# Opening steps in a fixed engine order, and attention steps in pairs over two MLP tasks, in a fused attention and two-MLP kernel

## The chip, the cores and the metric

One core of one Trainium2 chip runs the whole program. The metric is the device time of one execution in microseconds (us). TensorE multiplies matrices (PE in the rows; PEld is its loading of weights), VectorE is DVE, ScalarE is ACT, GpSimd is POOL, and SyncE (SP) issues most DMAs.

## What is computed

The reference, cut to what matters: sliding-window attention with a linear position bias, then an MLP with ELU, then an MLP with leaky ReLU, all in float32 (the weights arrive as 64-bit words).

```python
B, H, S, D = 4, 8, 576, 64
scores = q @ k.T / sqrt(D) + slope[h] * -|i - j|      # only 0 <= i - j < 128
attn = exp(scores - max); attn /= attn.sum() + 1e-9
x = (attn @ v)                                          # 2304 tokens x 512
h = x @ w_in;  g = where(h > 0, h, exp(min(h, 0)) - 1); x = g @ w_out     # 512 -> 2048 -> 512
h = x @ w_in2; g = maximum(0.01 * h, h);                out = g @ w_out2
```

## The kernel before, in words

**Attention steps.** The 2304 tokens are cut into nine blocks of 256, each block has four pairs of heads, and each pair of heads two steps (a tile of 128 queries, or two of 64): 72 steps. A step is a chain over all engines. TensorE makes the scores s_ps of both heads (`scores`, line 102 is the matmul helper). VectorE adds the bias and takes the row minimum of the negated scores in one pass per head (line 282), and folds the two halves of the window (line 294). ScalarE does the exponential with its sum (line 296). VectorE adds 1e-9 (line 299) and takes the reciprocal (line 300); POOL normalises t (line 302). TensorE transposes t (line 333, into pt_ps), ScalarE copies that to pt (line 338), POOL cuts the triangles out by two selects (lines 348, 350), and TensorE multiplies by v (`values`, av_ps). ScalarE then writes the high part of x (line 391) and VectorE the low part (line 392).

**The opening.** The first 16 steps (two blocks) run before any MLP work. In each, four warming products are issued ahead of the transposes, and the loop is `transposes(i)`, `values_to(i - 1)`, `scores(i + 2)`. At steps 6, 9, 12 and 15 `w_tick` adds a stage of weight conversion.

**Weights.** Each of the 16 pieces of a layer (wraw, 1 MB of 64-bit words) is turned into two float32r halves w in three stages: ScalarE splits off two words (lines 153, 154), VectorE shifts and adds them (lines 162, 163), ScalarE casts the high part (line 169), and VectorE and POOL subtract for the low part (line 173). One `w_tick` per task of the first block does the rest.

**First MLP.** It runs in blocks of 512, 256, 512, 512 and 512 tokens, of 16 tasks each. A task makes h_ps of one 128-wide chunk (`mlp1_h`: 12 products into the one bank of tag h), then ELU: an exponential on ScalarE (line 419), two VectorE operations (lines 420, 421, the second of which is the last to read the bank), a cast to gh (line 422) and a difference gl (line 424). Two tasks later `mlp1_y` multiplies by w_out (12 products, y). Beside each of the first four blocks run the attention steps of the next: 8 steps in the first block, 16 in each of the others; a step has `values` and `scores` ahead of the task's h and `transposes` behind it. Everything after that (last block, second MLP) has no attention.

**Who sets the order.** Matrix products, transposes and ScalarE's two first weight operations are kept in the order of the program. On the other engines a scheduler orders the instructions at build time by priority and estimated readiness; on the chip each engine works its list strictly one after the other. Banks are handed on by tag: the transposes and the values beside the MLP share one bank, c.

## Time and profile before

| | |
|---|---|
| median of 3 runs | 1001.73 us (1001.36 to 1003.89) |
| the profiled execution | 1004.1 us, its span 1002.4 us |
| busy of the span | PE 960.7 us, DVE 417.3, ACT 404.9, POOL 233.9 |
| opening | 0 to 70 us |
| first MLP, blocks 1 to 4 beside attention | 70 to about 520 us |

The span runs from the first to the last instruction of the program, and all times in the rows count from its start. TensorE's busy time is modelled from overlapping products, so a row of several products is best read by the distance to the start of the next row. Spans on POOL are rough. Idle time stands in brackets, with the instruction that ended it.

### The profile page before, as it was taken

How to read it: one execution, taken by the hardware profiler on the slowest of the kernel's cores; microseconds unless marked ns; L12 is line 12 of the kernel's file. 1: busy time of each engine (PE TensorE's matmuls, PEld its weight loads, DVE VectorE, ACT ScalarE, POOL GpSimd, SP SyncE). 2: the span in 40 equal slices, each digit the busy share in tenths (PEclk: the TensorE clock that was granted, in tenths of full speed). 3: DMA queues.
4: the chain of work that ended last, by engine and by line, in shares of the span. 5: the costliest groups of instructions: out<-in, count | busy, mean ns of one | idle time of the engine just before them, and what ended most of it. 6: DMA issues, size and time to landing. Idle time of an engine off the chain costs nothing.

```text
span 1002.4 us, 13318 instructions
## 1 busy us (share of the span) xinstructions
PE 960.7 (96%) x4885; PEld 754.8 (75%) x4885; DVE 417.3 (42%) x1050; ACT 404.9 (40%) x927; POOL 233.9 (23%) x393
## 2 busy tenths in 40 slices
PE   7778989989999999999999999999999999999998
PEld 4346767777777777777777888888888888888886
DVE  4558776454554444444437666621121121111111
ACT  3557665334443333433337566632231222212221
POOL 3465453233333432323313233200000000000000
PEclk9769998999999999999999999999999999999999
DMA  8732121121121111210042433510020001001001
GB/s 300 267 136 80 64 92 64 35 87 49 57 63 43 30 34 33 78 35 16 1 148 84 168 126 127 168 42 22 1 84 1 1 1 43 0 1 43 1 1 42
DMA packets 41617, 66.79 MB, mean 67 GB/s; under 512 B 3664, under 2 KB 26960, under 8 KB 41552
## 3 DMA queue, kind: packets, MB, share of 16 engines
q1 hardware_dynamic: 38704, 61.22, 18.2%
q10 hardware_dynamic: 2848, 4.72, 1.4%
q8 instruction: 38, 0.62, 0.3%
q14 instruction: 27, 0.22, 0.1%
HBM read 56.49 MB, written 9.44 MB: 66 GB/s over the span
## 4 chain that ended last, share of the span: by engine, by line
PE 83%; DVE 7%; ACT 4%; POOL 2%; issue 2%; DMA 0%; ACTq 0%; DVEq 0%; POOLq 0%
PE h_ps L102 36%; PE o_y L102 17%; PE y L102 16%; PE av_ps L102 5%; PE s_ps L102 4%; PE pt_ps L333 2%; DVE t L282 2%; POOL t L302 2%; DVE w L173 1%; ACT wf L153 1%; DVE eg L420 1%; PE o_s L102 1%; PE o_c L102 1%; ACT wraw L154 1%; ACT t L296 1%
## 5 line engine op out<-in xcount | busy, mean ns | idle before, releaser
L102 PE MATMUL h_ps<-x,w 128*128 128x512 f32 (+1 forms) x1920 | 434.1, 376 | 12.1 <-DVE eg L421 10.6
L102 PEld LDWEIGHTS h_ps<-x,w 128*128 128x128 f32 x1920 | 337.2, 190 | 90.4 <-issue 13.6
L543 DVE TENSOR_TENSOR g2l<-g,g2h 128x512 fp32r<-128x512 f32 (+1 forms) x80 | 52.1, 652 | 268.6 <-ACT g2h L542 268.6
L102 PE MATMUL y<-gh,w 128*128 128x512 f32 (+1 forms) x640 | 162.9, 377 | 0.0
L102 PE MATMUL o_y<-w,g2h 128*128 128x512 f32 x512 | 157.7, 389 | 0.0
L538 ACT ACTIVATE g<-h_ps 128x512 f32<-128x512 f32 (+1 forms) x80 | 44.3, 553 | 252.1 <-PE h_ps L102 250.9
L102 PEld LDWEIGHTS y<-gh,w 128*128 128x128 f32 x640 | 110.8, 189 | 18.3 <-DVE ys L446 0.4
L302 POOL TENSOR_SCALAR t<-t,stat 128x128 f32<-128x128 f32 (+3 forms) x160 | 64.0, 413 | 213.1 <-DVE stat L300 126.4
L102 PEld LDWEIGHTS o_y<-w,g2h 128*128 128x128 f32 x512 | 96.2, 188 | 20.0
L102 PE MATMUL o_y<-w,g2l 128*128 128x512 f32 x256 | 99.7, 389 | 0.0
L296 ACT ACTIVATE t<-t,stat 128x128 f32<-128x128 f32 (+3 forms) x160 | 62.9, 394 | 79.8 <-DVE t L294 64.9
L424 POOL TENSOR_TENSOR gl<-eg,gh 128x256 fp32r<-128x256 f32 (+1 forms) x80 | 70.6, 883 | 102.8 <-ACT gh L422 90.9
L422 ACT CAST gh<-eg 128x512 fp32r<-128x512 f32 (+1 forms) x80 | 46.1, 577 | 91.1 <-DVE eg L421 91.1
L102 PE MATMUL y<-gl,w 128*128 128x512 f32 (+1 forms) x320 | 79.0, 369 | 0.0
L420 DVE TENSOR_SCALAR eg<-eg 128x512 f32<-128x512 f32 (+1 forms) x80 | 51.5, 643 | 55.7 <-ACT eg L419 55.2
L282 DVE CUSTOM_DVE_ANT_0 t<-s_ps,bias 128x256 f32<-128x256 f32 (+4 forms) x160 | 54.4, 373 | 42.1 <-PE s_ps L102 37.9
L173 POOL TENSOR_TENSOR w<-wraw,w 128x512 fp32r<-128x512 f32 x32 | 53.6, 1677 | 67.2 <-ACT w L169 67.2
L102 PEld LDWEIGHTS y<-gl,w 128*128 128x128 f32 x320 | 56.9, 189 | 10.6
L419 ACT ACTIVATE eg<-h_ps 128x512 f32<-128x512 f32 (+1 forms) x80 | 44.1, 551 | 48.7 <-PE h_ps L102 46.0
L102 PE MATMUL av_ps<-pt,vr 128*64 128x128 f32 (+2 forms) x464 | 52.8, 279 | 6.3 <-POOL pt L348 5.9
L102 PEld LDWEIGHTS o_y<-w,g2l 128*128 128x128 f32 x256 | 48.0, 188 | 9.9
L102 PEld LDWEIGHTS av_ps<-pt,vr 128*64 128x64 f32 (+1 forms) x464 | 31.5, 135 | 31.7 <-issue 17.5
(56 smaller groups left out, 816.8 us busy)
## 6 DMA issues: line engine op xcount, KB each, us to landing
wraw<-in_w_in SPq DMA_DIRECT2D x32, 512.0 KB, 3.6
wraw<-in_w_out SPq DMA_DIRECT2D x32, 512.0 KB, 4.6
qkr<-in_kT SPq DMA_DIRECT2D x28, 192.0 KB, 2.5
x2T<-ys ACTq DMA_DIRECT2D x18, 256.0 KB, 2.5
out<-os SPq DMA_DIRECT2D x18, 256.0 KB, 2.1
xr<-x2T SPq DMA_DIRECT2D x4, 1024.0 KB, 5.4
qkr<-in_qT SPq DMA_DIRECT2D x28, 128.0 KB, 2.1
vr<-in_vp SPq DMA_DIRECT2D x16, 192.0 KB, 2.5
```

The source lines that it names most:

```text
L102: tc.keep_in_program_order(nc.tensor.matmul(*args, **kw))
L173: eng.tensor_tensor(w[:, io, 1], f[:, io], w[:, io, 0].bitcast(F32), op=ALU.subtract)
L282: nc.vector.tensor_tensor_reduce(out=t[:n, c], in0=ps[hh][:n, pc], in1=bias8[:n, 2 * p + hh, P - before:P + n], scale=-D ** -0.5, scalar=3 ...
L296: nc.scalar.activation(t[:n, c], t[:n, c], AF.Exp, scale=-1.0, bias=stat[:n, 0, i:i + 1], accum_out=stat[:n, 1, i:i + 1])
L302: nc.gpsimd.tensor_scalar(t[:n, c], t[:n, c], stat[:n, 2, i:i + 1], 1.0, op0=ALU.mult, op1=ALU.mult)
L333: tc.keep_in_program_order(nc.tensor.transpose(ps[:nk, col:col + n], t[:n, c:c + nk], ident[:n, :n]))
L419: nc.scalar.activation(g[:, :m], ps, AF.Exp)
L420: nc.vector.tensor_scalar(g[:, :m], g[:, :m], 1.0, -1.0, op0=ALU.min, op1=ALU.add)
L422: nc.scalar.copy(hi[:, :m], g[:, :m])
L424: eng.tensor_tensor(lo[:, half], g[:, half], hi[:, half].bitcast(F32), op=ALU.subtract)
L538: nc.scalar.activation(g, ps, AF.Prelu, alpha=0.01)
L543: nc.vector.tensor_tensor(lo, g, hi.bitcast(F32), op=ALU.subtract)
```

## The change

`Ordered` wraps ScalarE, VectorE and POOL: while its flag is on (the opening), what they issue is kept in the order of the program. `scores` is cut into `score_mm`, `score_min`, `score_exp`, `score_rec` and `score_norm`, and the selects and the writing of x become functions of their own. The opening's loop issues these in a fixed order, with the scores three steps ahead and the reciprocal of one step between the two score passes of the next; there the 1e-9 is added on ScalarE. Three weight pieces are converted at steps given by a table, `EARLY`. Beside the MLP two steps form a pair over two tasks: values and scores of both in front of the first task, the first step's transposes behind its h, the second step's transposes in front of the second task's h. Scores of both steps share the banks s0 and s1, values of both the bank c, and x is written 256 wide. q and k have two buffers instead of three, t has four instead of three.

```diff
-W_FROM = 6
+EARLY = [(2, "a1", 0), (3, "a2", 0), (3, "ts", 0), (4, "add", 0), (5, "hi", 0), (6, "lo", 0),
+         (6, "a1", 1), (7, "a2", 1), (7, "ts", 1), (8, "add", 1), (9, "hi", 1), (10, "lo", 1),
+         (10, "a1", 2), (11, "a2", 2), (11, "ts", 2), (12, "add", 2), (13, "hi", 2), (14, "lo", 2)]
...
+                ins = f(*args, **kw)
+                if Ordered.on:
+                    tc.keep_in_program_order(ins)
...
-    rawp = attn.enter_context(tc.tile_pool(name="raw", bufs=3))
-    tp_ = attn.enter_context(tc.tile_pool(name="tp", bufs=3))
+    rawp = attn.enter_context(tc.tile_pool(name="raw", bufs=2))
+    tp_ = attn.enter_context(tc.tile_pool(name="tp", bufs=4))
...
+        for i, (t0, n, before, hh, c, pc) in enumerate(st["reg0"]):
+            dve.tensor_tensor_reduce(
+                out=t[:n, c], in0=st["ps"][hh][:n, pc], in1=bias8[:n, 2 * st["p"] + hh, P - before:P + n],
+                scale=-D ** -0.5, scalar=3.0e38, op0=ALU.add, op1=ALU.min, accum_out=stat[:n, 0, i:i + 1])
+            if i == 0:
+                between()
...
+        if Ordered.on:
+            act.activation(stat[:nq, 1, :m], stat[:nq, 1, :m], AF.Copy, bias=1e-9)
+        else:
+            dve.tensor_scalar(stat[:nq, 1, :m], stat[:nq, 1, :m], 1e-9, None, op0=ALU.add)
...
+    def scores(k):
+        if 2 * k >= NS:
+            return
+        ps = score_mm(2 * k)
+        score_mm(2 * k + 1, ps, BLK)
+        for s in (2 * k, 2 * k + 1):
+            score_min(s)
+            score_exp(s)
+            score_rec(s)
+            score_norm(s)
...
-    for i in range(FIRST):
-        transposes(i)
-        values_to(i - 1)
-        scores(i + 2)
-        if i >= W_FROM and i % 3 == W_FROM % 3:
-            w_tick(NC)
+    for n in range(FIRST):
+        m = n + 2
+        transposes(n)
+        values_to(n - 1)
+        if n + 3 < FIRST + 2:
+            score_mm(n + 3)
+        if n >= 2:
+            values_out(n - 2)
+        score_min(m, lambda: score_rec(m - 1))
+        score_norm(m - 1)
+        score_exp(m)
+        selects(n)
+        w_early(n)
...
+        todo = NPAIR * (t0 + n) // BLK - done
+        starts = [i * NC // todo + (NC // todo - 2) // 2 for i in range(todo)]
         for c in range(NC):
-            step = (c + 1) * left // NC > c * left // NC
-            if step or c == 0:
-                values_to(done - 1)
-            if step:
-                scores(done + 2)
+            if c == 0 or c in starts:
+                values_to(2 * done - 1)
+            if c in starts:
+                scores(done + 1)
+            elif c - 1 in starts:
+                transposes(2 * done + 1)
+                selects(2 * done + 1)
+                done += 1
             g = mlp1_h(J, [c])
-            if step:
-                transposes(done)
-                done += 1
+            if c in starts:
+                transposes(2 * done)
+                selects(2 * done)
```

How the order moves, at three places. VectorE in the opening, around the first writing of x, before (line 282 is the score pass and its read of the minimum, 299 and 300 the constant and the reciprocal of the step before, 392 the low part of x):

```order
L282 ISA t,stat<-s_ps,bias_87 128x128
L282 ISA stat 128x1
L282 ISA t,stat<-s_ps,bias_87 128x128
L282 ISA stat 128x1
L299 TENSOR_SCALAR stat<-stat 128x2
L300 RECIPROCAL stat<-stat 128x2
L392 TENSOR_TENSOR x_264<-av_ps,x_264 128x256
```

The same place now (line 110 is the wrapper, whatever the operation):

```order
L110 ISA t,stat<-s_ps,bias_87 128x128
L110 ISA stat 128x1
L110 RECIPROCAL stat<-stat 128x2
L110 ISA t,stat<-s_ps,bias_87 128x128
L110 ISA stat 128x1
L110 TENSOR_TENSOR x_263<-av_ps,x_263 128x256
```

The reciprocal has moved up between the two passes, and the addition of the constant has left VectorE.

TensorE in the second, 256-wide block, one step before:

```order
L102 MATMUL av_ps<-pt,vr 64x128 x4
L102 MATMUL s_ps<-qkr 128x128 x2
L102 MATMUL h_ps<-x_902,w_11_1360 128x256 x12
L333 MATMUL pt_ps<-ident,t 128x128 x2
...
L102 MATMUL y_1903<-gh,w_8_1149 128x256 x2
L102 MATMUL av_ps<-pt,vr 64x128 x4
```

and a pair of steps now:

```order
L119 MATMUL av_ps<-pt,vr 64x128 x8
L119 MATMUL s_ps<-qkr 128x256 x2
L119 MATMUL s_ps<-qkr 128x128 x2
L119 MATMUL h_ps<-x_998,w_8_1197 128x256 x12
L413 MATMUL pt_ps<-ident,t 128x128 x2
...
L119 MATMUL y_1890<-gh,w_6_1103 128x256 x2
L413 MATMUL pt_ps<-ident,t 128x128 x2
L119 MATMUL h_ps<-x_998,w_9_1240 128x256 x12
```

Values and scores of two steps stand together, the second step's transposes stand ahead of the second h, and an h and a y follow before the next values.

ScalarE in the same block, one step before (391 is the cast of x, 419 the exponential of h, 338 the copy of the transposes):

```order
L391 CAST x_1770<-av_ps 128x128
L296 ACTIVATE t,stat<-t,stat 128x128 x2
L419 ACTIVATE eg<-h_ps 128x256
L338 COPY pt<-pt_ps 128x256
L422 CAST gh<-eg 128x256
```

and a pair now:

```order
L110 CAST x_1815<-av_ps 128x256
L110 ACTIVATE t,stat<-t,stat 128x128 x4
L507 ACTIVATE eg<-h_ps 128x256
L110 COPY pt<-pt_ps 128x256 x2
L510 CAST gh<-eg 128x256
L507 ACTIVATE eg<-h_ps 128x256
```

Four exponentials of the pair stand ahead of the exponential of h, and both copies follow it.

## Rows read from the trace of the kernel before

**Rows 1.** Windows: stretch, us, busy us of PE, PEld, DVE, ACT, POOL, clock.

```profile
7.50:70.00 62.50, 48.96 (x272) 26.79 (x272) 30.20 (x134) 31.66 (x102) 31.09 (x62) 0.75 0.66 239
70.00:189.80 119.80, 109.92 (x522) 82.39 (x521) 84.67 (x161) 72.75 (x140) 52.27 (x62) 0.95 0.23 76
189.80:275.00 85.20, 78.17 (x595) 64.33 (x593) 42.69 (x175) 35.06 (x130) 28.30 (x72) 1.00 0.21 63
275.00:520.00 245.00, 245.00 (x1306) 183.33 (x1306) 109.42 (x365) 92.40 (x284) 79.82 (x159) 1.00 0.15 45
```

**Rows 2.** Waits of TensorE over the span: us in total, times, longest.

```profile
PE pt_ps L333 <- POOL t L302: 14.5, 13, 2.2
PE h_ps L102 <- DVE eg L421: 10.6, 7, 2.4
```

**Rows 3.** Timeline, TensorE, opening: start us, us, what [idle before].

```profile
24.68 0.61 PE L102 MATMUL pt_ps<-ident 128*128 128x256 bf16 x4
25.13 0.65 PE L333 MATMUL pt_ps<-ident,t 128*128 128x128 f32 x2
25.70 0.76 PE L102 MATMUL av_ps<-pt,qkvr 128*64 128x128 f32 x8
26.39 0.70 PE L102 MATMUL s_ps<-qkvr 64*128 64x256 f32 x4
...
46.82 1.13 PE L102 MATMUL av_ps<-pt,qkvr 128*64 128x128 f32 x8
```

**Rows 4.** Timeline, ScalarE, opening.

```profile
25.87 0.37 ACT L338 COPY pt<-pt_ps 128x256 f32<-128x256 f32 x1 [1.66 <-PE pt_ps L333]
26.16 0.40 ACT L296 ACTIVATE t<-t,stat 128x128 f32<-128x128 f32 x1
...
26.94 0.35 ACT L391 CAST x<-av_ps 128x256 fp32r<-128x256 f32 x1
...
30.83 1.11 ACT L153 ACTIVATE wf<-wraw 128x1024 f32<-128x1024 f32 x1
```

**Rows 5.** Timeline, VectorE, opening.

```profile
28.07 0.40 DVE L392 TENSOR_TENSOR x<-av_ps,x 128x256 fp32r<-128x256 f32 x1
...
30.82 0.42 DVE L282 CUSTOM_DVE_ANT_0 t<-s_ps,bias 128x256 f32<-128x256 f32 x1 [2.02 <-PE s_ps L102]
...
31.98 0.16 DVE L300 RECIPROCAL stat<-stat 128x2 f32<-128x2 f32 x1
```

**Rows 6.** Timeline, POOL, opening.

```profile
24.67 0.72 POOL L302 TENSOR_SCALAR t<-t,stat 128x128 f32<-128x128 f32 x2
...
30.23 0.41 POOL L348 TENSOR_SCALAR_AFFINE_SELECT pt<-pt 128x256 f32<-128x256 f32 x1 [0.92 <-ACT pt L338]
...
32.31 0.99 POOL L302 TENSOR_SCALAR t<-t,stat 128x128 f32<-128x128 f32 x2 [1.20 <-DVE stat L300]
...
59.65 2.40 POOL L302 TENSOR_SCALAR t<-t,stat 128x128 f32<-128x128 f32 x2 [2.03 <-ACT wraw L154]
```

**Rows 7.** Timeline, TensorE, first MLP block: its start, two startup waits, dearest product row.

```profile
70.04 4.09 PE L102 MATMUL h_ps<-x,w 128*128 128x512 f32 x12
...
76.80 3.06 PE L102 MATMUL h_ps<-x,w 128*128 128x512 f32 x12 [2.08 <-DVE eg L421]
...
82.62 3.67 PE L102 MATMUL h_ps<-x,w 128*128 128x512 f32 x8 [2.39 <-DVE eg L421]
...
151.50 5.49 PE L102 MATMUL h_ps<-x,w 128*128 128x512 f32 x12 [1.84 <-DVE eg L421]
```

**Rows 8.** Timeline, TensorE, one step of the 256-wide block.

```profile
218.98 1.69 PE L102 MATMUL h_ps<-x,w 128*128 128x256 f32 x12
220.50 0.38 PE L333 MATMUL pt_ps<-ident,t 128*128 128x128 f32 x2
220.64 0.72 PE L102 MATMUL y<-gh,w 128*128 128x256 f32 x4
...
223.06 1.13 PE L102 MATMUL av_ps<-pt,vr 128*64 128x128 f32 x8 [0.74 <-POOL pt L348]
```

More of the change, by code (lines that the diff above doesn't have):

```diff
@@ L46 @@
 LAG2 = 4
-def pair_of(steps, pairs, s):
-    st = steps[min(s, len(steps) - 1)]
-    return pairs.index((st["j"], st["p"]))
 def slope(h):
@@ L99, in attention_elu_leaky_kernel, with __init__, __getattr__, call @@
     nc = tc.nc
+    class Ordered:
+        on = False
+        def __init__(self, eng):
+            self.eng = eng
+        def __getattr__(self, name):
+            f = getattr(self.eng, name)
+            def call(*args, **kw):
+                ins = f(*args, **kw)
+                if Ordered.on:
+                    tc.keep_in_program_order(ins)
+                return ins
+            return call
+    act, dve, pool = Ordered(nc.scalar), Ordered(nc.vector), Ordered(nc.gpsimd)
     def matmul(*args, **kw):
@@ L255, in prep, with score_mm @@
             ahead["load"] += 1
-    def scores(s):
-        if s >= NS:
-            return
+    def score_mm(s, ps=None, at_=0):
         st = steps[s]
@@ L279, in scores, with score_min @@
             at_ += w
-        for i, (t0, n, before, hh, c, pc) in enumerate(reg):
-            nc.vector.tensor_tensor_reduce(
-                out=t[:n, c], in0=ps[hh][:n, pc], in1=bias8[:n, 2 * p + hh, P - before:P + n], scale=-D ** -0.5,
-                scalar=3.0e38, op0=ALU.add, op1=ALU.min, accum_out=stat[:n, 0, i:i + 1])
+        st["ps"], st["reg0"] = ps, reg
+        return ps
+    def score_min(s, between=lambda: None):
+        st = steps[s]
+        t = tp_.tile([P, 512], F32, tag="t", name="t")
+        stat = tp_.tile([P, 3, 4], F32, tag="stat", name="stat")
+        st["t"], st["stat"] = t, stat
+        for i, (t0, n, before, hh, c, pc) in enumerate(st["reg0"]):
[4 more added lines that the diff above has]
+                between()
@@ new lines, in score_rec, with score_norm @@
+    def score_rec(s):
+        st = steps[s]
+        nq, m = st["subs"][0][1], len(st["reg"])
+        dve.reciprocal(st["stat"][:nq, 2, :m], st["stat"][:nq, 1, :m])
+    def score_norm(s):
+        st = steps[s]
+        t, stat = st["t"], st["stat"]
+        for i, (t0, n, before, hh, c) in enumerate(st["reg"]):
+            pool.tensor_scalar(t[:n, c], t[:n, c], stat[:n, 2, i:i + 1], 1.0, op0=ALU.mult, op1=ALU.mult)
+    def scores(k):
[8 more added lines that the diff above has]
+            score_norm(s)
@@ L337, in transposes, with selects @@
             c = slice(g[0][0].start, g[-1][0].stop)
-            nc.scalar.copy(pt[:nk, c], ps[:nk, c])
+            act.copy(pt[:nk, c], ps[:nk, c])
+        st["groups"], st["col"] = groups, col
+    def selects(s):
+        if s >= NS:
+            return
+        st = steps[s]
+        pt, groups, col = st["pt"], st["groups"], st["col"]
         for (nk, m), g in groups.items():
@@ L367, in values @@
         xh, xl = X1[J]
-        whole = j < RAW
+        early = j < RAW
         pt = st["pt"]
         tiles = [x for x in st["reg"] if x[3] == 0]
-        if not whole:
-            av, off = psp.tile([P, 512], F32, tag="c", name="av_ps"), -j * BLK
-        elif st["first"]:
-            av, off = psp.tile([P, 512], F32, tag=f"y{p % 2}", name="av_ps"), -j * BLK
-            AV[p] = av
-        else:
-            av, off = AV[p], -j * BLK
+        if st["first"]:
+            AV[p] = psp.tile([P, 512], F32, tag=f"y{p % 2}" if early else "c", name="av_ps")
+        av, off = AV[p], -j * BLK
         for t0, n, before, _, _ in tiles:
@@ L386, in values, with values_out @@
                                      start=i == 0, stop=i == len(mine) - 1)
-        if whole and not st["last"]:
+        st["out"] = None
+        if st["last"]:
+            o = slice(j * BLK - BLK1[J][0], j * BLK + BLK - BLK1[J][0])
+            st["out"] = xh[:, p, o], xl[:, p, o], av[:, :BLK]
+    def values_out(s):
+        if s >= NS or not steps[s]["out"]:
             return
-        a, b = (j * BLK, j * BLK + BLK) if whole else (tiles[0][0], tiles[-1][0] + tiles[-1][1])
-        q, o = slice(a + off, b + off), slice(a - BLK1[J][0], b - BLK1[J][0])
-        nc.scalar.copy(xh[:, p, o], av[:, q])
-        nc.vector.tensor_tensor(xl[:, p, o], av[:, q], xh[:, p, o].bitcast(F32), op=ALU.subtract)
+        xh, xl, av = steps[s]["out"]
+        act.copy(xh, av)
+        dve.tensor_tensor(xl, av, xh.bitcast(F32), op=ALU.subtract)
     def mlp1_h(J, cs):
```

116 lines of the change are left out of this document (74 added, 42 removed).

## The prediction

> **What bounds the kernel now.** I read the stages first, then the waits, then the timeline of each engine inside the stages. The windows by stage [rows 1] show where TensorE is not busy: it is idle for 62.5 - 48.96 = 13.5 us of the opening (7.5 to 70 us, sixteen attention steps), 119.8 - 109.92 = 9.9 us of the first MLP block (70 to 189.8), 85.2 - 78.17 = 7.0 us of the second, 256-wide block (189.8 to 275), and never between 275 and 520. Behind 520 us the change moves nothing. So at most some 30 us are open, plus what the clock takes: the granted clock is 0.75 of 2.4 GHz in the opening, that is half of it at 1.2 GHz, and 0.95 in the first block. The waits of TensorE [rows 2] name who ends the idle time: the normalising on POOL before the transposes (opening), and the maximum on VectorE that frees the one bank of h_ps (first block).
>
> **The opening, priced as a loop.** The order listing shows what is cured: before, VectorE does the +1e-9 and the reciprocal of a step behind the next step's two score passes, which wait for that step's products. In the new order the products come a step earlier, the constant is added on ScalarE, and the reciprocal stands between the two passes. What remains is a ring of fixed orders; I add up two steps, because the output copy of a pair comes every second one, and call one trip a turn.
>
> *Ring through TensorE:* transposes to the copy's start 25.87 - 25.13 = 0.74 [rows 3, 4]; copy 26.16 - 25.87 = 0.29, x cast 0.35 [rows 4]; x subtraction 0.40, score pass 0.42 [rows 5]; reciprocal to normalising 32.31 - 31.98 = 0.33, normalising 0.72, first select 0.41 [rows 5, 6]; values 26.39 - 25.70 = 0.69, scores 0.70, the four warming products 25.13 - 24.68 = 0.45 [rows 3], and the transposes again: 5.50 us, 2.75 a step.
> *Ring through ScalarE:* copy 0.29, cast 0.35, x subtraction 0.40, pass, reciprocal, pass and minimum at 0.42 + 0.16 + 0.42 + 0.42, two exponentials 26.94 - 26.16 = 0.78, the added constant, then reciprocal, pass, minimum, exponentials and constant of the second step. The minimum has no row here and is taken as a pass. The 128x2 addition on ScalarE has none either: between 0 and the 0.40 of an exponential [rows 4], I take 0.2, being nearer to the small end by width. Sum: 3.44 + 1.98 = 5.42 us. (The Trainium skill, "ScalarE: Activation LUTs", section "What ACT_TABLE_LOAD costs", puts an ACTIVATE with immediate operands at 186 ns plus 0.833 ns per element, 0.19 us here; the sum would be the same within 0.2 us. No run here shows it yet.)
> *Weights:* nine ScalarE stages of 1.11 us [rows 4] are put at fixed steps, after the exponentials. Where one falls into the odd step only, the second copy comes 0.4 us later, and the turn is 5.8; where both steps have one (steps 5/6 and 9/10), 6.9. The stages on VectorE and POOL stand behind their step's work and are hidden by the wait for the next products; if that cover goes, they come on top (second rival).
>
> So: first transposes at 7.5 us as before, three steps at 2.75 to step 3 (15.8), six turns (4 x 5.8 + 2 x 6.9 = 37.0) to step 15 (52.8), then one last way through copy, cast, subtraction, pass, reciprocal, double normalising of the 64-row step, selects and values: 0.74 + 0.29 + 0.35 + 0.40 + 0.42 + 0.33 + 1.44 + 0.82 + 0.69 = 5.5. The first MLP product starts at 58.3 us at full clock, against 70.04 [rows 7]. At half clock values take 1.13 instead of 0.76 [rows 3]; with as much for scores and warming, a turn grows by 1.1: eight turns at that give 65. I put the clock where it was, half the time, and 1 us for passes that meet on SBUF: **62 us, -8** (bounds -11.7 and -5). The weights at hand are then three whole pieces, where before two were whole and two half done.
>
> **First MLP block.** Two startup waits of 2.08 and 2.39 us [rows 7] stay: in both orders six exponentials and two weight passes stand on ScalarE ahead of the second task's exponential. The other 9.9 - 4.5 = 5.4 us come where VectorE and ScalarE have a step's scores and a weight piece at once; the new order has four such places instead of eight, but after eight of its tasks nothing but y lies between h and the next h. I take half, 2.7 us. A clock of 0.95 over 119.8 us is worth 6.0 us of TensorE work; the dearest product row, 5.49 us for twelve products, is such a stretch behind a wait [rows 7]. With half the waits gone I give back somewhat under half: **-5** together. Bounds: -11 (both gone but the startup) and +3.1 (eight tasks with 5.4 / 14 = 0.39 us each, the mean wait of a task behind the startup, on top of what there is).
>
> **Second, 256-wide block.** Today each step's values wait 0.74 us for the select [rows 8], as only y lies between. Now h and y lie between the second step's transposes and the values, 1.52 (218.98 to 220.50) + 1.68 (220.64 to 223.06 less its wait) = 3.2 us [rows 8], so that wait goes. What is late next: ScalarE has one queue, and in most pairs four exponentials now stand ahead of exp(h), whose maximum frees the h bank. From the end of the scores: four passes and two minima on VectorE 6 x 0.42 = 2.5, the second pair of exponentials 0.78, exp(h) at most 0.40, two VectorE passes 0.84: 4.5 us. TensorE comes back to that bank after h, transposes, y, transposes: 1.52 + 0.14 + 1.68 + 0.14 = 3.5 us [rows 8]. So up to 1.0 us a pair; in some pairs a score is only 128 wide, in some the order puts exp(h) first: I take 0.6 of the 0 to 1.0, 4.8 us for eight pairs against 7.0 today: **-2** (bounds -7 and +1).
>
> **275 to 520 us.** TensorE is always busy [rows 1]; in these 512-wide tasks y alone covers the chain. Values and scores of two steps now run together: two changes between products and attention less per pair. One change costs between 0 and 0.14 us (the whole spacing of a transpose pair [rows 8]); 16 pairs: 0 to -4.5, **-1.5** taken.
>
> **No cost.** Two buffers for q and k instead of three: a pair's loads on SP now wait for scores that were read a whole pair earlier, and land during the two tasks between; on SP the sixteenth weight piece moves ahead of the eleventh and twelfth, which are used ten tasks and more later. The fourth buffer of t only removes waits. The x copies are half as many and twice as wide, off the path of the products.
>
> Sum: -8 - 5 - 2 - 1.5 = -16.5. The profiled execution took 1004.1 us (span 1002.4) and lies 2.4 above the median of the three runs, 1001.7; I subtract from the median: **985.2 us**.
>
> **Rivals.**
> 1. *Everything comes in:* full clock in the opening (-11.7), no wait behind the startup in the first block (-9), the h bank always in time (-6), changes at 0.09 us (-3): 972. For it: a shorter turn has fewer gaps, and the granted clock is 1.00 where TensorE is always busy [rows 1]. Against: the granted 0.75, in an opening with TensorE 78% busy. 20%.
> 2. *POOL and VectorE in each other's way:* POOL's normalising takes 0.72 us undisturbed and 2.40 beside weight work on VectorE [rows 6]. Three pieces have six such VectorE stages (add, subtraction); if each meets a normalising in the ring, 6 x 1.68 = 10 us: the opening ends at 72, the sum is 995. Against: the stages stand where the next normalising is not due. 15%. (The Trainium skill says in "GPSIMD Engine Reference", section "Specifications", that POOL shares its SBUF interfaces with VectorE and that instructions with two SBUF inputs contend; by that rule this is what the added piece would do. The trace agrees, 2.40 beside 0.72.)
> 3. *The pair gives back what the opening wins:* in the 256-wide block the passes, both pairs of exponentials and the two reciprocals run strictly one behind the other, 2.0 us a pair: 16 instead of 7, +9; the first block gains nothing: 1001, no change. 8%.
> 4. *Slower: a fixed order exposes every weight stage.* On queues that no longer choose, a stage that is not ready holds all behind it. Nine ScalarE stages are 10 us, the nine on VectorE bounded by the same; on half-clock turns of 6.6: 7.5 + 8 x 6.6 + 20 + 5.5 = 86 us, +16, with the rest as forecast 1009. It decides from an opening longer than 78.5 us. For it: these engines were free to be ordered around a late stage before, and from then on are not. Against: ScalarE is busy for 31.66 of the 62.5 us only [rows 1], so there is room for a late stage to be made good. 9%.
>
> That the change does not do what it says is excluded by the order: it shows both the ring and the pairs.
>
> **Numbers.** The forecast has 48%. A measurement tells about 0.3% (3 us) from no change: faster 48 + 20 + 15 and 1 from the third, 0.84; same 0.07; slower 0.09. The range reaches from below rival 1 by its unknown costs to just over rival 3: 967 to 1003, which leaves out rival 4 and the far ends. The forecast's own range, each term moved by about half of the way to its bounds, is 976 to 993.
>
> **What would show it.** Right: first MLP product near 62 us; pairs of steps 5.5 to 7 us apart in the opening, with the wait for POOL under 8 us; no wait of av_ps for POOL in the 256-wide block, and in its place h_ps waiting for VectorE under 1 us a pair. Wrong: an opening over 66 us with normalising at 1.4 us and more (rival 2), h_ps waits of 2 us a pair (rival 3), ScalarE idle ahead of a weight stage (rival 4), or waits in the 512-wide blocks, where I expect none.

## The result: 966.6 us, and the profile after

The changed kernel takes **966.62 us** (median of 4 runs, 966.46 to 968.23), the kernel before 1002.78 us (4 runs, 1001.36 to 1003.89): ratio 0.9644, 95% interval 0.9625 to 0.9663. The gain is 36 us where 16.5 were forecast; the time lies 0.4 us below the range. The profiled execution took 966.66 us, its span is 964.8. The medians below leave out one execution of e16 at 1045.2 us and one of the kernel before at 1855.5, far above the others.

The windows of the changed kernel, cut where its stages begin (columns as in [rows 1]: stretch, us, busy us of PE, PEld, DVE, ACT, POOL, clock); the last one holds the two 512-wide blocks with attention.

```profile
7.50:60.10 52.60, 40.94 (x267) 23.30 (x267) 28.38 (x113) 34.11 (x121) 31.05 (x61) 0.90 0.91 315
60.10:171.20 111.10, 106.12 (x525) 81.39 (x524) 84.22 (x158) 73.50 (x136) 51.87 (x61) 0.97 0.20 65
171.20:245.90 74.70, 71.61 (x595) 63.24 (x593) 40.95 (x166) 33.18 (x122) 28.92 (x72) 1.00 0.25 72
245.90:470.30 224.40, 223.99 (x1250) 174.92 (x1248) 99.09 (x336) 84.84 (x258) 77.81 (x156) 1.00 0.13 39
```

The last of these windows in the kernel before, same columns:

```profile
274.90:507.80 232.90, 232.90 (x1254) 173.33 (x1252) 103.96 (x353) 87.89 (x274) 78.09 (x157) 1.00 0.12 36
```

The opening is shorter by 9.9 us (the start of the first product of the MLP, from here on the opening's mark, is 60.1 for 70.0), the first block by 8.6 (111.1 for 119.7), the 256-wide block by 10.5 (74.7 for 85.2), and the two 512-wide blocks, in which TensorE showed no idle time at all, by 8.4 (in the kernel before they end at 507.8 us, inside the last window of [rows 1]). The waits of TensorE over the span answer to [rows 2]:

```profile
PE pt_ps L413 <- POOL t L110: 8.7, 13, 1.8
PE h_ps L119 <- DVE eg L509: 5.0, 10, 1.3
PE pt_ps L413 <- ACT pt L110: 4.4, 3, 2.5
PE av_ps L119 <- POOL pt L110: 3.0, 1, 3.0
```

The wait for the normalising fell by 5.8 us and that for the bank of h by 5.6; the wait for ScalarE's copies is new. The wait of the values for the selects, not among [rows 2], fell by 3.8. In the kernel before it was:

```profile
PE av_ps L102 <- POOL pt L348: 6.8, 9, 0.9
```

Together that is 15.2 us less and 4.4 more, far from 36. The timeline of TensorE in the 256-wide block shows what else changed (answers to [rows 8]):

```profile
198.57 0.64 PE L119 MATMUL y<-gh,w 128*128 128x256 f32 x4
199.14 1.15 PE L119 MATMUL av_ps<-pt,vr 128*64 128x128 f32 x16
200.22 0.92 PE L119 MATMUL s_ps<-qkr 64*128 64x256 f32 x8
201.07 1.69 PE L119 MATMUL h_ps<-x,w 128*128 128x256 f32 x12
```

Sixteen value products now take 1.08 us (199.14 to 200.22). Before, eight took 1.06 there (223.06 [rows 8] to the next start, 224.12), and 0.60 in the block's second task, where y was 512 wide (200.40 to 201.00):

```profile
200.40 0.67 PE L102 MATMUL av_ps<-pt,vr 128*64 128x128 f32 x8
201.00 0.70 PE L102 MATMUL s_ps<-qkr 64*128 64x256 f32 x4
...
224.12 0.70 PE L102 MATMUL s_ps<-qkr 64*128 64x256 f32 x4
```

### The profile page after: what moved, and what is told of

The parts are those of the page before. It is cut to its first block, busy times and chain, and to the rows that moved or that the text cites. A ratio compares the mean times of both kernels' runs of the same rounds, so it can differ in the third digit from the quotient of the medians.

```text
span 964.8 us, 13200 instructions
## 1 busy us (share of the span) xinstructions
PE 934.1 (97%) x4885; PEld 751.3 (78%) x4885; DVE 408.9 (42%) x1003; ACT 403.0 (42%) x917; POOL 234.6 (24%) x393
## 4 chain that ended last, share of the span: by engine, by line
PE 80%; DVE 3%; ACT 3%; issue 1%; DMA 0%; ACTq 0%; DVEq 0%
PE h_ps L119 37%; PE o_y L119 18%; PE y L119 16%; PE av_ps L119 4%; PE s_ps L119 3%; ACT t L110 1%; PE o_s L119 1%; PE pt_ps L413 1%; PE o_c L119 1%; DVE t L110 1%; DVE eg L508 1%; DVE eg L509 1%; ACT wraw L174 0%; ACT wf L169 0%; DVE stat L110 0%
## 5 line engine op out<-in xcount | busy, mean ns | idle before, releaser
L659 DVE TENSOR_TENSOR g2l<-g,g2h 128x512 fp32r<-128x512 f32 (+1 forms) x80 | 52.1, 653 | 268.9 <-ACT g2h L658 268.9
L119 PE MATMUL y<-gh,w 128*128 128x512 f32 (+1 forms) x640 | 160.0, 372 | 0.0
L512 POOL TENSOR_TENSOR gl<-eg,gh 128x256 fp32r<-128x256 f32 (+1 forms) x80 | 68.2, 852 | 139.8 <-ACT gh L510 132.0
L110 POOL TENSOR_SCALAR t<-t,stat 128x128 f32<-128x128 f32 (+3 forms) x160 | 65.7, 424 | 136.3 <-DVE stat L110 130.0
L508 DVE TENSOR_SCALAR eg<-eg 128x512 f32<-128x512 f32 (+1 forms) x80 | 46.8, 586 | 94.4 <-ACT eg L507 91.1
L110 ACT ACTIVATE t<-t,stat 128x128 f32<-128x128 f32 (+3 forms) x160 | 62.5, 392 | 55.2 <-DVE t L110 40.4
L512 DVE TENSOR_TENSOR gl<-eg,gh 128x256 fp32r<-128x256 f32 (+1 forms) x80 | 41.6, 521 | 39.0 <-ACT gh L510 38.8
L509 DVE TENSOR_TENSOR eg<-h_ps,eg 128x512 f32<-128x512 f32 (+1 forms) x80 | 51.1, 638 | 2.7
```

The source lines that it names most:

```text
L110: ins = f(*args, **kw)
L119: tc.keep_in_program_order(nc.tensor.matmul(*args, **kw))
L508: nc.vector.tensor_scalar(g[:, :m], g[:, :m], 1.0, -1.0, op0=ALU.min, op1=ALU.add)
L509: nc.vector.tensor_tensor(g[:, :m], ps, g[:, :m], op=ALU.max)
L512: eng.tensor_tensor(lo[:, half], g[:, half], hi[:, half].bitcast(F32), op=ALU.subtract)
L659: nc.vector.tensor_tensor(lo, g, hi.bitcast(F32), op=ALU.subtract)
```

## Experiments

All stages in us, read from TensorE's timeline: the start of the first product (the opening's end), the first block, the 256-wide block, the two 512-wide blocks; then the median time. The ratios in the text are each to executions of the kernel before taken beside the run (medians 1001.2 to 1003.1 us). The diffs are shortened, with some lines joined.

| run | opening | first | 256 | 512 x 2 | time |
|---|---|---|---|---|---|
| before | 70.0 | 119.7 | 85.2 | 232.9 | 1002.8 |
| changed | 60.1 | 111.1 | 74.7 | 224.5 | 966.6 |
| e1 pairs only | 65.6 | 111.4 | 74.6 | 224.5 | 974.0 |
| e2 opening only | 60.0 | 117.8 | 83.8 | 232.9 | 994.4 |
| e3 second select aside | 65.1 | 121.6 | 80.4 | 232.1 | 995.3 |
| e4 interleaved | 61.6 | 110.8 | 78.7 | 227.2 | 974.1 |
| e5 transposes behind | 59.6 | 115.6 | 73.7 | 224.8 | 971.5 |
| e6 transposes together | 60.9 | 111.6 | 76.8 | 232.5 | 977.9 |
| e7 buffers only | 66.1 | 121.4 | 84.4 | 232.9 | 1002.5 |
| e8 last select first | 60.2 | 109.4 | 74.7 | 224.5 | 964.9 |
| e9 before again | 65.7 | 119.7 | 85.3 | 232.9 | 1001.3 |
| e10 not pinned | 53.4 | 111.2 | 74.7 | 224.6 | 960.5 |
| e11 reciprocal behind | 62.5 | 111.4 | 74.7 | 224.5 | 969.3 |
| e12 copies behind | 59.8 | 111.1 | 72.9 | 224.3 | 965.6 |
| e13 constant on ScalarE | 65.7 | 109.3 | 74.6 | 224.5 | 970.9 |
| e14 products earlier | 56.5 | 111.0 | 74.6 | 224.5 | 963.4 |
| e15 free, together | 52.9 | 110.1 | 72.8 | 224.2 | 959.3 |
| e16 one run | 52.1 | 109.9 | 79.6 | 225.4 | 964.1 |
| e17 x behind | 54.9 | 110.1 | 74.4 | 224.5 | 959.8 |
| e18 pinned, best | 52.0 | 109.6 | 72.8 | 224.3 | 955.3 |

**Which half gains what.** Two runs take the halves of the change apart. e1 has the scheduler's old opening, then the pairs:

```diff
-    Ordered.on = True
-    ...
+    for i in range(FIRST):
+        transposes(i); selects(i); values_to(i - 1); score_one(i + 2)
+        if i >= 6 and i % 3 == 0:
+            w_tick(NC)
```

> The pairs of steps beside the MLP with the opening as it was before (scheduler's order, weight stages from step 6 on, +1e-9 on VectorE). Theory (the parts are separate): the first MLP product stays near 70 us, and the 256-wide block (-10.5 us), the two 512-wide blocks behind it (-8.5 us) and the first block (-8.6 us) gain as in the changed kernel: about 974 us. Rival (the first block gained because the new opening leaves three whole pieces of weights and a tidy start): of the 8.6 us only the fewer changes of four pairs, some 2 us, are left: about 981 us. The forecast's own terms would have given 1002 - 5 - 2 - 1.5 = 993 us.

Measured: 974.0 us, 0.9721 (0.9698 to 0.9743). e2 has the new opening, then the old loop of single steps:

```diff
-            if c in starts:
-                scores(done + 1)
+            if step:
+                score_one(done + 2)
             g = mlp1_h(J, [c])
+            if step:
+                transposes(done); selects(done); done += 1
```

> The new opening, then one attention step at a time beside the MLP, as before. Theory (separate parts): first MLP product at 60 us instead of 70, all behind it as before: 1002.8 - 10 = 993 us. Rival (the first block's gain comes from the opening): a further 6 us, 987 us. The forecast's own term was -8: 995 us.

Measured: 994.4 us, 0.9927 (0.9896 to 0.9959). The first theory holds: the halves are separate, and the pairs bring 27.5 us of the 36. Most of the first block's gain goes with the pairs too: 111.4 with the old opening, 117.8 with the new one alone.

**The 256-wide block.** In e3 the kernel before keeps its two selects, but the second writes where nobody reads (so a mask is left out), and nothing waits for it:

```diff
-            nc.gpsimd.affine_select(out=both, in_=both, pattern=[[0, 2], [1, n]], base=0,
+            aside = tp_.tile([P, 2 * P], BF16, tag="aside", name="aside", bufs=1)
+            nc.gpsimd.affine_select(out=aside[:, :w]..., in_=both, pattern=[[0, 2], [1, n]], base=0,
```

> The kernel before, in which the second select writes to a tile that nobody reads: the products of the values wait for the first select alone, and POOL has the same work. The mask of the tokens after a query is left out by this. Theory (a wait for the second select hides inside the rows of the values, which look busy): in the 256-wide block the rows of 8 value products shrink from 1.07 to about 0.60 us (start to next start), about 0.45 us in 14 of 16 steps, -6 us; in the 512-wide blocks, where the 8 take 0.59 us already, nothing; in the opening up to 0.4 us a step of the ring, 0 to -6 us: 990 to 997 us. Rival (values cost more there for another reason, such as what the products before them were): no row changes, 1002 us within 0.3%.

Measured: 995.3 us, 0.9933 (0.9908 to 0.9957), and 4.8 of it in this block (85.2 to 80.4). The timeline of e3, one step of the block:

```profile
242.59 0.67 PE L102 MATMUL av_ps<-pt,vr 128*64 128x128 f32 x8 [0.76 <-POOL pt L348]
243.18 0.49 PE L102 MATMUL s_ps<-qkr 64*128 64x128 f32 x4
```

The wait of 0.76 us for the first select is still there; the eight products behind it now take 0.59 us, not 1.06. The row that looked busy held a wait of 0.47 us for the second select, which follows the first on POOL. The trace of the kernel before had it too, not in TensorE's products but in its weight loading: at 223.53 in the row of [rows 8], when POOL's second select (223.08, 0.41 us) is done, and 3.1 us in 11 places of the block:

```profile
223.08 0.41 POOL L350 TENSOR_SCALAR_AFFINE_SELECT pt<-pt 128x256 f32<-128x256 f32 x1
223.06 0.19 PEld L102 LDWEIGHTS av_ps<-pt,vr 128*64 128x64 f32 x2 [0.95 <-POOL pt L348]
223.53 0.42 PEld L102 LDWEIGHTS av_ps<-pt,vr 128*64 128x64 f32 x6 [0.28 <-POOL pt L350]
...
PEld av_ps L102 <- POOL pt L350: 3.1, 11, 0.4
```

(The Trainium skill says in "Perfetto Trace Analysis", section "Summary: the profiler window per engine type", that the end shown for a TensorE instruction is an estimate. The trace agrees: these eight products look busy for 1.13 us with that wait and for 0.67 without it.)

**The 512-wide blocks.** e4 alternates values and scores in each pair; no place of attention is added between the products of the MLP:

```diff
-                values_to(2 * done - 1)
-                scores(done + 1)
+                values_to(2 * done - 2); ps = score_mm(2 * done + 2)
+                values_to(2 * done - 1); score_mm(2 * done + 3, ps, BLK)
```

> The changed kernel, in which the values and the score products of a pair alternate step by step (values, scores, values, scores) instead of 16 value products and then 8 score products; the number of places where attention stands between products of the MLP is the same. Theory J (every change between kinds of matmul costs): two more changes a pair; by the rows of the changed kernel 8 values cost 0.59 us at the start of a run and 0.48 behind 8 others, 4 scores 0.64 and 0.42: +0.32 us a pair, 28 pairs, +9 us: 975.5 us. Rival (only the changes between the MLP's products and attention cost): no difference, 966.6 us within 0.3%.

Measured: 974.1 us, 0.9721 (0.9700 to 0.9743): 7.5 us lost. One pair of e4's 512-wide blocks:

```profile
274.71 0.66 PE L119 MATMUL av_ps<-pt,vr 128*64 128x128 f32 x8
275.30 0.70 PE L119 MATMUL s_ps<-qkr 64*128 64x256 f32 x4
275.93 0.67 PE L119 MATMUL av_ps<-pt,vr 128*64 128x128 f32 x8
276.53 0.70 PE L119 MATMUL s_ps<-qkr 64*128 64x256 f32 x4
```

and of the changed kernel:

```profile
269.31 1.15 PE L119 MATMUL av_ps<-pt,vr 128*64 128x128 f32 x16
270.38 1.14 PE L119 MATMUL s_ps<-qkr 64*128 64x256 f32 x8
271.44 3.04 PE L119 MATMUL h_ps<-x,w 128*128 128x512 f32 x12
```

The same 24 matmuls take 2.45 us alternating (to 277.16) and 2.13 in two runs. That is 2.7 of the 8.4 us in the two blocks (and as much in the 256-wide one, beside 1.4 us more of listed waits); 16 pairs of the kind shown would give 5.1, so the other kinds gain less. The other 5.7 us lie between e2 and e4 (232.9 and 227.2): one run of values and scores fewer a pair, 0.36 us. Part of it was hidden waits here too, 0.8 us by e3 (232.9 to 232.1). The rows of pairs like the one above give the rest of the split: two steps take 14.33 us before (values at 293.27 to values at 307.60), a pair of e4 14.08 (274.71 to 288.79), a changed pair 13.76 (269.31 to 283.07). So one place of attention fewer is worth 0.25 us, and the grouping in the place that stays 0.32; an estimate for 16 pairs is 4.0 us for the places, and 0.9 of the 5.7 stays open.

**Where the second step's transposes stand.** e5 puts them behind the second task's first products:

```diff
-                transposes(2 * done + 1)
             g = mlp1_h(J, [c])
+            if c - 1 in starts:
+                transposes(2 * done + 1)
```

> The changed kernel with the second step's transposes behind the first products of the second task (as the first step's are) instead of ahead of them. Only y then lies between these transposes and the values. Theory (what the place ahead of the products buys is the cover for the selects): in the 256-wide block each pair waits again for the first select, 0.74 us, and for the second, 0.47 us, 8 pairs: up to +9.7 us; in the 512-wide blocks y takes 2.8 us and covers the chain: 0; the wait of 2.48 us at the first pair behind the opening goes: -2.5. Sum 966.6 + 7 = 974 us. Rival (the pair alone is enough, since the selects of the second step are queued on a freer POOL): 964 to 967 us.

Measured: 971.5 us, 0.9709 (0.9687 to 0.9732). Of the theory only the sum was near: the 256-wide block is 1.0 us *shorter* and no wait for a select is listed in it (one row of sixteen values takes 1.30 us, the others 1.07). So it is not h between the transposes and the values that ends that wait; the pair is enough. The loss is in the first block (115.6 for 111.1). Over the span the waits of h for VectorE are

```profile
PE h_ps L119 <- DVE eg L509: 13.6, 15, 3.4
```

against 5.0 us in the changed kernel; 8.8 us of them stand in the first block, where the changed kernel has 2.5. e6 puts the transposes of both steps into one run and one bank, where they fit:

```diff
-                transposes(2 * done + 1)
+                transposes(2 * done + 1, transposes(2 * done), width(2 * done))
```

> The changed kernel with the transposes of both steps in one run into one bank, ahead of the second task's products, where they fit the bank (20 of 28 pairs). Theory J (every place where attention stands between the products costs beside its own matmuls): by the rows of the changed kernel y behind transposes takes 2.92 us and 2.81 without, h before them 2.88 and 2.84: -0.15 us a pair, 20 pairs, -3 us, and the two waits of 0.9 us for the copy out of the transposes' bank in the 256-wide block go: -5 us in all, 961.6 us. Rival (two copies and four selects now stand between the transposes and the values, 0.6 + 1.6 us and more against 3.2 us of products in the 256-wide block, so the values wait again, up to 0.5 us in six pairs): no gain, 964 to 967 us.

Measured: 977.9 us, 0.9768 (0.9749 to 0.9786), worse by 11 us, which neither theory had. Its waits name a new one: the second step's transposes wait for the first step's copy out of the shared bank, queued on ScalarE.

```profile
PE pt_ps L419 <- ACT pt L110: 15.6, 21, 2.5
```

e12 gives the two copies out behind both runs of transposes:

```diff
-                    transposes(2 * done + 1, transposes(2 * done), width(2 * done))
+                    transposes(2 * done + 1, transposes(2 * done, alone=False), width(2 * done), alone=False)
+                    copies(2 * done); copies(2 * done + 1)
```

> The transposes of both steps in one run into one bank as in the run before, but with the two copies out of the bank given out behind both runs of transposes: there the second step's transposes waited 15.6 us in all for the first step's copy on ScalarE, which lies in the same bank. Theory J (one place less where attention stands between products gains 0.25 us, as h and y gained 4.0 us for 16 pairs of the two 512-wide blocks): those waits go, 20 pairs gain 0.15 to 0.25 us each, -3 to -5 us: 961.6 to 963.6 us, the two 512-wide blocks 221.5 to 222.7 us instead of 224.5. Rival (the values now wait for copies and selects that start later): 966 us or more, with waits of the values for POOL in the 256-wide block.

Measured: 965.6 us, 0.9644 (0.9623 to 0.9665). Those waits are gone (2.5 us are left, the one at the start); 1.8 us come in the 256-wide block, and in the 512-wide ones 0.2, not 2 to 3; the interval of the whole overlaps that of the changed kernel. Joining two places of transposes gains next to nothing: the first four products of y take 1.01 us behind transposes and 0.91 elsewhere, but four transposes in one run take 0.35 us, and two runs of two 0.13 and 0.14. Theory J holds for values and scores, not for these.

**The opening.** First, how firm its length is: e7 is the kernel before with the change's buffers, e9 the kernel before unchanged.

```diff
-    rawp = attn.enter_context(tc.tile_pool(name="raw", bufs=3))
-    tp_ = attn.enter_context(tc.tile_pool(name="tp", bufs=3))
+    rawp = attn.enter_context(tc.tile_pool(name="raw", bufs=2))
+    tp_ = attn.enter_context(tc.tile_pool(name="tp", bufs=4))
-            vr = rawp.tile([P, 4, P], F32, tag="vr", name="vr")
+            vr = rawp.tile([P, 4, P], F32, tag="vr", name="vr", bufs=3)
```

> The kernel before with the buffers of the change alone: four for t, two for q and k, three for v. In the run with pairs and the old opening the first product of the MLP started at 65.6 us, not at 70. Theory (the fourth buffer of t, which the prediction booked as removing waits at no gain, shortens the old opening, since a step's scores no longer wait for the transposes of the step three before): first product near 65.5 us, 997.5 us. Rival (the buffers change nothing; the scheduler ordered that opening otherwise because other work follows it): first product at 70 us, 1001.6 us within 0.3%.

> The kernel before once more, for its profile. In its profile the granted clock was 0.74 to 0.53 between 30 and 66 us and the first product of the MLP came at 70 us; with the buffers alone changed it was 1.00 up to 40 us and 66.1 us, at the same time of the whole. Theory (the opening before has no fixed length: how long the clock stays at half differs from one execution to the next): first product between 65 and 70 us, with a granted clock unlike that of the first profile in the opening, everything behind 190 us the same within 1 us. Rival (70 us belongs to the kernel before and 66 to the buffers): 70 us again, within 1 us.

Measured: e7 1002.5 us, 1.0009 (0.9989 to 1.0028); e9 1001.3 us, with the first product at 65.7. The buffers gain nothing. Each stage behind the opening repeats to 0.2 us, the opening itself only to 4.3: its granted clock was 0.75 [rows 1] and in the second execution

```profile
7.50:65.70 58.20, 42.49 (x272) 23.63 (x272) 30.23 (x134) 31.65 (x102) 31.24 (x62) 0.87 0.74 258
```

So the new opening is worth 5.6 to 9.9 us by its marks, 7.2 by the medians of e2 (in whose profile the first and the 256-wide block are 3.3 us shorter too). Four runs look for its cause. e10 removes the pins:

```diff
                 ins = f(*args, **kw)
-                if Ordered.on:
-                    tc.keep_in_program_order(ins)
```

> The changed kernel with the opening's instructions given out in the same sequence, but not held in it: the scheduler may order ScalarE, VectorE and POOL in the opening, as in the kernel before (+1e-9 stays on ScalarE there). Theory (the fixed order is what shortens the opening): first product at 65 us or later, some 5 us lost, 971 us and more. Rival (the products of a step earlier and the added constant on ScalarE do it, and the scheduler keeps it): first product at 60 us, 966.6 us within 0.3%.

e11 moves the reciprocal behind both passes and the minimum:

```diff
-            if i == 0:
-                between()
         st["reg"] = []
         ...
+        between()
```

> The changed kernel with the reciprocal of a step behind both score passes and the minimum of the next step on VectorE, not between the passes; the rest of the fixed order stays. Theory (the ring of the prediction: normalising waits for the reciprocal, and so for 0.42 + 0.42 us more in each step that the ring through TensorE ends): +0.84 us in each of 13 to 16 steps less what the ring through ScalarE covers, +6 to +12 us, first product at 66 to 72 us, 973 to 978 us. Rival (the ring through ScalarE or the weights set the pace): under +2 us.

Measured: e10 **960.5 us**, 0.9594 (0.9569 to 0.9620), 6.1 us *faster* than with the fixed order, which neither theory had; e11 969.3 us, 0.9678 (0.9660 to 0.9700), 2.7 us slower than the changed kernel, between theory and rival. e13 and e14 then add to e1 one part of the new sequence each, unpinned:

```diff
-        if Ordered.on:
+        if s < FIRST + 2:
             act.activation(stat[:nq, 1, :m], stat[:nq, 1, :m], AF.Copy, bias=1e-9)
```

> The run with pairs and the old opening (974.0 us, first product at 65.6), with one part of the new opening added: +1e-9 on ScalarE for the opening's steps, nothing pinned. Theory (what gains is the products of the scores a step earlier; the constant only spares VectorE a small operation): 0 to -3 us, first product at 63 to 66 us. Rival (the constant on VectorE, behind the next step's passes, is what held the normalising): first product at 57 us or earlier, 965 us.

```diff
+        if i + 3 < FIRST + 2:
+            score_mm(i + 3)
         score_one(i + 2)
```

> The run with pairs and the old opening (974.0 us, first product at 65.6), with the other part: the score products of the opening are issued one step earlier, the constant stays on VectorE, nothing pinned. Theory: -8 to -12 us, first product at 54 to 58 us, 962 to 966 us, near the run without pins (53.4 us). Rival (the products earlier gain nothing without the constant and the order on VectorE): 972 to 974 us.

Measured: e13 970.9 us, 0.9680 (0.9645 to 0.9716), 3.1 us by medians with the opening's mark unmoved and intervals that overlap; e14 963.4 us, 0.9611 (0.9581 to 0.9641): **the score products a step earlier gain 10.6 us**. VectorE's wait for score products in the opening says why: 18.3 us in e1, 6.2 in e14. In the kernel before it was

```profile
DVE t L282 <- PE s_ps L102: 29.1, 15, 3.4
```

and in that of the changed kernel, first VectorE, then ScalarE, what the fixed order put in its place:

```profile
DVE x L110 <- ACT x L110: 12.1, 6, 3.6
DVE stat L110 <- ACT stat L110: 5.0, 8, 1.0
DVE x L110 <- PE s_ps L119: 2.2, 1, 2.2
DVE t L110 <- PE s_ps L119: 0.8, 1, 0.8
...
ACT t L110 <- DVE t L110: 11.7, 8, 1.7
```

VectorE hardly waits for score products any more (the 2.2 us put down to them end at 43.72, just as ScalarE's cast of x from 43.30 does), but stands in front of the pinned subtraction of x until ScalarE has cast x, while the next step's scores are ready; ScalarE then waits for those passes. The timeline of ScalarE shows one turn: a weight stage, the copy, the cast, and then the wait.

```profile
28.13 1.12 ACT L169 ACTIVATE wf<-wraw 128x1024 f32<-128x1024 f32 x1
29.15 0.35 ACT L110 COPY pt<-pt_ps 128x256 f32<-128x256 f32 x1
29.40 0.37 ACT L110 CAST x<-av_ps 128x256 fp32r<-128x256 f32 x1
31.50 0.40 ACT L110 ACTIVATE t<-t,stat 128x128 f32<-128x128 f32 x1 [1.72 <-DVE t L110]
```

e17 leaves everything pinned and moves x behind the passes and exponentials:

```diff
-        if n >= 2:
-            values_out(n - 2)
         score_min(m, lambda: score_rec(m - 1))
         score_norm(m - 1)
         score_exp(m)
+        if n >= 2:
+            values_out(n - 2)
```

> The changed kernel, opening still pinned, with the cast and the subtraction of x of a finished pair behind the next step's score passes and exponentials, not ahead of them. Theory (the fixed order costs because VectorE stands before the subtraction of x, 12.1 us in six places, while the next step's scores are ready): that wait falls under 3 us, first product at 53 to 55 us instead of 60.1, 960 to 962 us. Rival (the weight stages of 1.1 us pinned ahead of the transposes' copies on ScalarE set the pace): the wait moves to another place, first product at 58 us or later, 964.5 us and more.

Measured: 959.8 us, 0.9572 (0.9552 to 0.9593), first product at 54.9: time and mark as the theory had them, its wait not. VectorE still waits 12.0 us for that cast, but no longer ahead of the passes. Shorter are ScalarE's wait in the opening and, over the span, TensorE's for the normalising (8.7 before this edit); its wait for selects grows from 3.0 to 4.5:

```profile
ACT t L110 <- DVE t L110: 6.7, 9, 1.0
...
PE pt_ps L413 <- POOL t L110: 4.2, 7, 1.4
```

**A version that beats both.** e8 gives the opening's last selects out ahead of the normalising of step 16:

```diff
+        if n == FIRST - 1:
+            selects(n)
         score_norm(m - 1)
         score_exp(m)
-        selects(n)
+        if n < FIRST - 1:
+            selects(n)
```

> The changed kernel with the selects of the opening's last step ahead of the normalising of step 16 on POOL. At the end of the opening TensorE waits 2.98 us for that select. Theory (it waits because the normalising of step 16, which nobody needs before the second task, and the exponentials it waits for stand ahead of the select): -2 to -2.9 us, first product at 57.5 to 58 us, 964 us. Rival (the select waits for the copy on ScalarE, which stands behind the exponentials itself): the wait stays, 966.6 us.

Measured: 964.9 us, 0.9636 (0.9620 to 0.9653); the wait of 2.98 us at the opening's end shrinks to 1.0. The opening's mark doesn't show it; TensorE's clock was 0.84 and 0.77 from 40 to 50 and 50 to 58 us of this execution, and 1.00 in the changed kernel's. By the medians it is 1.8 us, with intervals that overlap. In this profile the difference stands in the first block (109.4 for 111.1); why, no run shows. e15 joins this and the transposes of e12 to e10, e18 joins e8, e12 and e17, pinned (the run before, in its expectation, is e17). e16 is e15 with the transposes right behind the scores:

```diff
             if c in starts:
                 scores(done + 1)
+                if together(done):
+                    transposes(2 * done + 1, transposes(2 * done, alone=False), width(2 * done), alone=False)
+                    ...
             elif c - 1 in starts:
-                if together(done):
-                    ...
```

> The changed kernel without pins, with the transposes of both steps in one run (copies behind both), and the selects of the opening's last step given out first. Theory (the parts add up: no pins 960.5, transposes together -1.0, the last selects 0 to -1.5 since the wait left there is 1.6 us): 958 to 959.5 us. Rival (the opening's end is set by the scheduler's own order, and what the transposes gain in the 256-wide block comes back as waits of h): 960.5 us within 0.2%.

> As the run before, but values, scores and both transposes of a pair stand in one run ahead of the first task's products, where they fit the bank (20 of 28 pairs). Theory J (one more place between products goes; in the run with the copies behind, one place of transposes less was worth 0.0 us a pair in the 512-wide blocks): 0 to -2 us beside the run before. Rival (the transposes wait: for the bank, which the copy of the values' result must leave, 0.7 us and more after the values against 1.06 us of score products, and in the 256-wide block for a normalising that is one task less old): 0.3 to 1.5 us a pair in the eight pairs of the 256-wide block, +3 to +12 us.

> As the run before, with the last selects of the opening first and the transposes of both steps in one run. Theory: the run before less 1.0 (transposes) less 0 to 2 (the last selects): 957 to 960 us, level with the best run without pins (959.3 us). Rival: the run before within 0.3%.

Measured: e15 959.3 us, 0.9568 (0.9544 to 0.9592); e16 964.1 us, 0.9620 (0.9593 to 0.9648), the 256-wide block at 79.6 as its rival had it, with

```profile
PE pt_ps L417 <- DVE x L110: 4.8, 7, 1.9
```

e18 **955.3 us** (954.56 to 957.26, 4 runs), 0.9533 (0.9506 to 0.9560): the best, 11 us below the changed kernel and below what its theory had. Its executions all lie below those of e15 (958.16 to 959.58), though the intervals of the ratios overlap. So a fixed order need not lose, once x stands in the right place; the same sequence without the pins was not run.

## Why the prediction was wrong, point by point

The sign, the places and the opening's size were right; the forecast failed in two terms, the 256-wide block and the 512-wide blocks, which gained 8.5 and 6.9 us more than forecast, and by 3.6 in the first block.

*Opening, -8:* 5.6 to 9.9 by the marks, 7.2 by e2. The size holds, the reason only in part. "VectorE does the +1e-9 and the reciprocal of a step behind the next step's two score passes, which wait for that step's products": the products a step earlier gain 10.6 us (e14), the reciprocal's place 2.7 (e11), and the constant is not told from nothing by the mark. The rings held the cast and the subtraction of x ahead of the passes as given; that this place is itself a cost of the fixed order, 6.9 us by e17, was not priced. In part the size is luck. The clock was 0.90, not the 0.75 of the sum. The six turns from step 3 (transposes at 13.83) to step 15 (54.13) took 8.2, 5.6, 8.3, 5.6, 7.2 and 5.4 us: 6.7 on average, where the sum had 6.2 at full clock, and the long ones begin at steps 3, 7 and 11, not at the weights of 5/6 and 9/10. And eight turns of 1.1 us on top of 58.3 are 67.1, not the 65 of the bound. The addition on ScalarE, priced at 0.2 us, took 204 ns on average. (The Trainium skill, "ScalarE: Activation LUTs", section "What ACT_TABLE_LOAD costs", gives an ACTIVATE with immediate operands 186 ns plus 0.833 ns per element, 188 here as an estimate; the trace agrees within 16 ns.)

```profile
L110 ACT ACTIVATE stat<-stat 128x2 f32<-128x2 f32 x17 | 3.5, 204 | 0.5
```

*First block, -5:* 8.6. TensorE's idle time in it fell from 9.9 to 5.0 us, where 2.7 of 9.9 were taken, and its busy time by 3.8; the clock rose from 0.95 to 0.97 and four pairs group their products, and which of the two did how much is not shown. That two startup waits stay was half right: 0.76 us for 2.08 [rows 7], and in place of the 2.39 another, 2.48 us of the transposes for ScalarE's copy.

*256-wide block, -2:* 10.5. The step that failed is "each step's values wait 0.74 us for the select": the second select was left out of the sum, though POOL's own row showed 0.41 us for one [rows 6]. It stood inside a busy row (4.8 us, e3). The listed waits, summed over the block's rows, fell from 6.6 to 3.0. Those of h for VectorE are 0.8 us of it, so the 4.8 us set against the gain for the h bank was also too much. The grouping gave 2.7 more, which had no term.

*275 to 520 us, -1.5:* 8.4, beyond the bound of -4.5. The step that failed is "One change costs between 0 and 0.14 us (the whole spacing of a transpose pair [rows 8])". That prices a place of transposes, but the place that goes is one of values and scores, worth 0.25 us a pair by the rows above where 0.09 was taken. And the grouping of products of a kind inside the place that stays, 0.32 us in such a pair and 2.7 in all (e4), had no term. "TensorE is always busy [rows 1]" hid another 0.8 us of waits (e3).

*No cost:* right for the buffers (e7).

*Rivals:* the first, "everything comes in", was nearest with 972 us, though not by its parts: the opening's clock was 0.90, not full. The second, POOL and VectorE in each other's way, did not decide: two pairs of normalisings in the changed opening took 1.40 and 0.88 us (at 30.82 and 33.04), against 0.72 and 2.40 [rows 6], and the opening still ended at 60.1. The third did not come: h waits 0.2 us in four of the eight pairs of the 256-wide block. The fourth had a real mechanism, a fixed queue that holds what is ready, at 6 to 7 us, not 20.

*Signs:* the mark, the missing wait of the values for POOL in the 256-wide block and the short waits of h there came as named. The pairs of steps in the opening are 5.4 to 8.3 us apart, not 5.5 to 7, the wait for POOL is 8.7 us, not under 8, and the 512-wide blocks have one wait of 0.4 us.

Open is where 0.9 of the 5.7 us between e2 and e4 go, and why, in e5, the place of the transposes lengthens the first block and shortens the 256-wide one.

## What to carry to other kernels

A row of TensorE that is busy throughout can hold waits and changeover costs: compare the start-to-start time of the same row in a covered and an uncovered step, and read the waits of its weight loading, before taking "always busy" as a bound. Try matmuls of a kind in one run where their inputs allow it: here values and scores gained by it, transposes did not. Before pinning an order, list for each queue what stands ahead of the next step's critical instruction and what that waits for; here the output of a finished step belonged behind it.

## What the runs showed of the hardware

Worked out from the rows of a pair above: eight 128x128 value products take 0.59 us at the head of a run, the next eight 0.48 (1.07 less 0.59); four score products 0.63 and 0.43 (1.06 less 0.63). Four transposes in one run take 0.35 us (e12), two runs of two 0.13 and 0.14; the first products of y behind transposes take 0.10 us longer (1.01 for 0.91), so joining them gains next to nothing. The opening of one kernel ended 4.3 us apart in two executions, at a granted clock of 0.75 and 0.87, while the stages behind it agreed to 0.2 us.
